# Keys and queries of two batches turned by the DMA crossbar, four PSUM slots in the first MLP pass, and output matmuls handed out in another order

## The chip, the core and the metric

The kernel runs on one core of one Trainium2 chip. The core's engines each work through their own list of instructions in order, and wait for each other by semaphores: PE (TensorE, matmuls and transposes by matmul), DVE (VectorE), ACT (ScalarE), POOL (GpSimd, here mostly an issuer of DMAs and a helper for squares and copies) and SP (SyncE, an issuer of DMAs). The metric is the device time of one execution in microseconds; lower is better. Times quoted as "span" run from the first to the last instruction of the profiled execution.

## What is computed

Two stages, one after the other. First a chunked attention over k, q, v of shape (4 batches, 8 heads, 768 positions, 64): each chunk of 32 positions looks at 16 positions to its left, at itself, at 8 to its right, and at 8 memory positions of its batch and head. Then a two-layer MLP on the 3072 rows of 512 that come out:

```python
for c in range(nc):                       # chunks of 32, nc = 24
    k_full = concat([mem_k, k[max(0, 32c-16) : 32c+40]])
    scores = q_c @ k_full.T / sqrt(64)
    a = softmax(scores)
    out[32c : 32c+32] = a @ v_full
x = out.transpose(0, 2, 1, 3).reshape(3072, 512)
h = x @ w_in                              # 512 -> 2048
g = h + sin(alpha * h)**2 / alpha
return g @ w_out                          # 2048 -> 512
```

## The kernel before

**Layout of the attention.** A batch is worked in eight blocks `j` of 96 query positions (`QW`), that is three chunks. For a block, 120 key positions and the 8 memory keys stand beside each other as 128 columns of `kT` (head dimension on the partitions, two heads stacked). `scores` makes eight matmuls into `sc`, then three exponentials on ACT write `pt` with a mask in the bias; `values` makes eight matmuls with the rows `vw` of v into `ot` and DVE divides by the sum (`rinv`, `x_blk`); `turn_x` transposes the block on PE (`xtp`) and DVE copies it into `xT`. `attention` runs these as a pipeline of steps, with `values` lagging `scores` by `lag` steps, and after each piece takes a given number (`shares`) of matmuls from a `stream`.

**Keys and queries.** `load_qk` brings k and q of a batch as six consecutive positions per partition (`k_bf`, `q_bf`). For batches 1 to 3, POOL pairs two heads (`pair_up`, tile `pr`), PE transposes six 128x128 pieces (`turn`, tiles `tk` and `tq`), and `put_k` (ACT one copy, DVE two) or `put_q` (DVE one copy) spreads them into `kT` or `qT`. There are eight such pieces for a batch, four of k and four of q, numbered `pc`. In the pass of batch 0 they are made at tiles `ft` 8 to 15, in the passes of batches 1 and 2 at every second tile from 2, each for the batch that follows. `put_memk` adds the memory keys, `put_memv` the memory values (eight copies on POOL), `load_v` the rows of v (four DMAs issued by POOL). `kTs`, `qTs` and `vws` have two buffers, used by even and odd batches.

**The MLP.** For a batch there are 16 tiles `ft` of 128 hidden features. `first` makes eight matmuls into `hT`, and ACT takes the sine (`u`). The square `s2` (shown as `s` in the profile) is made on ACT, DVE or POOL: by the string `AVPAVPAVPAVPAVPA` in the first pass, by `AAAV` in the others. `finish` (DVE) writes `gT` and so frees the `hT` slot. `second` is a generator of 96 output matmuls for a batch (six row groups `o` of 16), each group copied to `o_sb` and stored by SP. Those 96 are the `stream`: they are made during the attention and the MLP pass of the next batch, wherever the code takes some.

**PSUM.** Pool `big` has three slots of two banks (for `sc`, `ot`, `hT`), pool `one` two slots of one bank (for `tk`, `tq`, `xtp`, `o`). A tile waits for its slot until the last reader of the slot's old tile is done.

**Order.** The schedule is manual: every engine's instructions stand in the order in which the code writes them. So each of the queues is a list fixed in advance, DMAs included, and the order of the code around the change decides what stands behind what. POOL issues nearly all loads, in the order of the code; a load also waits until the eighth load before it has landed.

The passes follow each other as attention 0, pass 0, attention 1, pass 1 and so on; at the end the 96 output matmuls of batch 3 stand alone.

Of the kernel before, what the change touches and what calls it, by code (L numbers as in the profile page):

```python
# [9 lines left out]
P = 128  # L10
QW = 96
NEG = -30000.0
KW = 856
# [6 lines left out]
class Stream:  # L20


    def __init__(self, gen, n):
        self.gen = gen
        self.left = n

    def take(self, n):
        n = min(n, self.left)
        for _ in range(n):
            next(self.gen)  # L30
            self.left -= 1
# [3 lines left out]
def kernel(  # L35
# [27 lines left out]
    xp = ctx.enter_context(tc.tile_pool(name="xp", bufs=2))  # L63
# [3 lines left out]
    big = ctx.enter_context(tc.tile_pool(name="big", bufs=3, space=bass.MemoryType.PSUM))  # L67
    one = ctx.enter_context(tc.tile_pool(name="one", bufs=2, space=bass.MemoryType.PSUM))

    ctx.enter_context(tc.manual_schedule())  # L70

# [8 lines left out]
    memv_st = consts.tile([P, B, H, D], BF, name="memv_st")  # L80
    memkT = consts.tile([P, HP, 32], BF, name="memkT")
# [8 lines left out]
    def alloc_qk():  # L90
        kb = qkst.tile([P, H, 6, D], BF, name="k_bf")
        qb = qkst.tile([P, H, 6, D], BF, name="q_bf")
        return kb, qb

# [18 lines left out]
    def put_memv(b):  # L113
        for h in range(H):
            nc.gpsimd.tensor_copy(  # L115
                vws[b % 2][64:72, h, :, 0:D],
                memv_st[64:72, b, h, :].unsqueeze(1).to_broadcast([NM, NJ, D]),
            )

    def put_memk(b):  # L120
        nc.vector.tensor_copy(  # L121
            kTs[b % 2][:, :, 24:KW].rearrange("p g (j c) -> p g j c", c=104)[:, :, :, 40:40 + NM],
# [3 lines left out]
    def load_w_in(c):  # L126
        nc.gpsimd.dma_start(  # L127
            w_in_sb[:, :, 256 * c:256 * c + 256],
            moe_w_in[:, 256 * c:256 * c + 256].rearrange("(kt p) f -> p kt f", p=P),
        )  # L130
# [9 lines left out]
    def pair_up(src, hp):  # L140
        pr = blk.tile([P, 6, 2, D], BF, name="pr")
# [5 lines left out]
    def turn(src, hp, pr, name):  # L147
        t = one.tile([P, 6, P], BF, name=name, tag="one")
# [33 lines left out]
    def scores(b, j):  # L182
        sc = big.tile([P, 2, 512], F32, name="sc", tag="big")
        for hp in range(HP):
            for e in range(2):
                nc.tensor.matmul(  # L186
                    sc[:, e, QW * hp:QW * hp + QW],
                    kTs[b % 2][64 * e:64 * e + 64, hp, 104 * j:104 * j + P],
# [17 lines left out]
    def values(b, j, pt):  # L206
        ot = big.tile([P, 2, 512], F32, name="ot", tag="big")
# [18 lines left out]
    def turn_x(xT, j, x_blk):  # L226
        xtp = one.tile([P, KT, QW], BF, name="xtp", tag="one")
# [23 lines left out]
    def first(ft, xT, gT, square):  # L251
        hT = big.tile([P, 2, 512], F32, name="hT", tag="big")
# [89 lines left out]
    for c in range(2, 8):  # L342
        load_w_in(c)
# [107 lines left out]
```

## Time and profile before

| | us |
|---|---|
| median of 3 runs (lowest to highest) | 270.76 (269.01 to 272.1) |
| the profiled execution's own time | 268.79 |
| its span | 267.0 |
| busy in the span: PE, DVE, ACT, POOL | 220.6, 145.2, 156.0, 86.7 |
| attention 0 with all loading ahead | 0 to 33.3 |
| pass 0 | 33.3 to 75.2 |
| attention 1, pass 1 | 75.2 to 97.3, 97.3 to 134.2 |
| attention 2, pass 2 | 134.2 to 152.8, 152.8 to 192.6 |
| attention 3, pass 3 | 192.6 to 210.9, 210.9 to 241.6 |
| output matmuls of batch 3 and the last store | 241.6 to 267.0 |

Matmuls overlap in their pipeline, so the busy time of PE overstates what it did, and the distance from one group of matmuls to the next says more than a single duration. The stages are cut at the first matmul of each on PE; the engines overlap at the seams. Mean granted TensorE clock is 0.962.

### The profile page before, as it was taken

How to read it: one execution, taken by the hardware profiler on the slowest of the kernel's cores; microseconds unless marked ns; L12 is line 12 of the kernel's file. 1: busy time of each engine (PE TensorE's matmuls, PEld its weight loads, DVE VectorE, ACT ScalarE, POOL GpSimd, SP SyncE). 2: the span in 40 equal slices, each digit the busy share in tenths (PEclk: the TensorE clock that was granted, in tenths of full speed). 3: DMA queues.
4: the chain of work that ended last, by engine and by line, in shares of the span. 5: the costliest groups of instructions: out<-in, count | busy, mean ns of one | idle time of the engine just before them, and what ended most of it. 6: DMA issues, size and time to landing. Idle time of an engine off the chain costs nothing.

```text
span 267.0 us, 4449 instructions
## 1 busy us (share of the span) xinstructions
PE 220.6 (83%) x1756; PEld 124.3 (47%) x1781; DVE 145.2 (54%) x271; ACT 156.0 (58%) x238; POOL 86.7 (32%) x114
## 2 busy tenths in 40 slices
PE   1745792297899999898499899999499999999994
PEld 1534551154545555454245555555245555554441
DVE  4524931457983656768727538675747465575100
ACT  2263753057577647977756487778657479773000
POOL 8879745545699201229820011210000000000000
PEclk9999979579999999999979999999979999999999
DMA  6999999999059990108997110110101111011222
GB/s 95 167 131 132 164 202 206 199 95 32 0 62 216 150 116 2 39 0 120 166 130 52 41 42 0 39 42 0 39 2 39 42 39 39 2 41 39 82 79 79
DMA packets 52037, 21.10 MB, mean 79 GB/s; under 512 B 34592, under 2 KB 48944, under 8 KB 52016
## 3 DMA queue, kind: packets, MB, share of 16 engines
q0 software_dynamic: 48240, 14.45, 81.7%
q1 hardware_dynamic: 3776, 6.37, 7.1%
q8 instruction: 14, 0.23, 0.4%
q14 instruction: 7, 0.06, 0.1%
HBM read 28.95 MB, written 6.29 MB: 132 GB/s over the span
## 4 chain that ended last, share of the span: by engine, by line
PE 58%; DVE 11%; POOL 9%; DMA 9%; ACT 7%; issue 4%; ACTq 0%; DVEq 0%; POOLq 0%
PE o L284 28%; PE hT L255 23%; DVE gT L273 6%; DMA q_bf<-in_q_dram 6%; POOL vw L115 3%; DMA vw<-in_v_dram 3%; PE sc L186 3%; ACT u L262 2%; ACT kT L161 2%; DVE qT L173 2%; PE xtp L229 2%; PE ot L212 2%; POOL w_in_sb L127 2%; POOL q_bf L97 1%; DVE kT L167 1%
## 5 line engine op out<-in xcount | busy, mean ns | idle before, releaser
L255 PE MATMUL hT<-xT,w_in_sb 128*128 128x384 bf16 x512 | 96.7, 335 | 15.5 <-DVE gT L273 15.1
L284 PE MATMUL o<-w_out_sb,gT 128*128 128x512 bf16 x359 | 98.1, 387 | 2.1 <-DVE o_sb L292 0.5
L262 ACT ACTIVATE u<-hT,alpha_sb 128x768 f32<-128x768 f32 x64 | 57.6, 900 | 48.3 <-PE hT L255 47.6
L273 DVE SCALAR_TENSOR_TENSOR gT<-s,inv_alpha,hT 128x768 bf16<-128x768 f32 x64 | 63.1, 1008 | 29.6 <-ACT s L267 16.6
L255 PEld LDWEIGHTS <-w_in_sb 128*128 128x128 bf16 x512 | 49.4, 100 | 55.1 <-issue 18.2
L199 ACT ACTIVATE pt<-sc,biasm 128x256 bf16<-128x256 f32 x96 | 38.3, 474 | 26.2 <-PE sc L186 26.0
L284 PEld LDWEIGHTS <-gT 128*128 128x128 bf16 x384 | 33.8, 98 | 30.2 <-issue 0.5
L267 ACT ACTIVATE s<-u 128x768 f32<-128x768 f32 x42 | 35.5, 845 | 1.0
L142 POOL COPY pr<-q_bf 128x768 bf16<-128x768 bf16 x12 | 9.9, 827 | 53.4 <-PE tk L151 50.2
L218 DVE RECIPROCAL rinv<-ot 96x8 f32<-96x8 f32 x32 | 6.5, 202 | 30.6 <-PE ot L212 30.3
L219 DVE TENSOR_TENSOR x_blk<-ot,rinv 96x512 bf16<-96x512 f32 x32 | 22.0, 686 | 1.1
L292 DVE COPY o_sb<-o 128x512 f32<-128x512 f32 x12 | 8.3, 690 | 21.2 <-PE o L284 21.0
L294 ACT COPY o_sb<-o 128x512 f32<-128x512 f32 x12 | 7.0, 586 | 21.5 <-PE o L284 13.1
L212 PE MATMUL ot<-vw,pt 128*128 128x65 bf16 x256 | 14.8, 204 | 5.5 <-POOL vw L115 3.1
L186 PE MATMUL sc<-qT,kT 64*128 64x96 bf16 x256 | 12.2, 226 | 8.3 <-DVE kT L121 8.3
L212 PEld LDWEIGHTS <-pt 128*128 128x128 bf16 x256 | 13.0, 104 | 12.9 <-DMA vw<-in_v_dram 3.5
L115 POOL COPY vw<-memv_st 8x512 bf16<-8x512 bf16 x32 | 18.0, 606 | 0.1
L161 ACT COPY kT<-tk 128x672 bf16<-128x672 bf16 x16 | 11.4, 715 | 9.9 <-PE tk L154 9.6
L173 DVE COPY qT<-tq 128x768 bf16<-128x768 bf16 x16 | 15.3, 954 | 3.4 <-PE tq L151 3.2
L167 DVE COPY kT<-tk 128x48 bf16<-128x48 bf16 x32 | 5.1, 202 | 21.7 <-ACT kT L161 21.7
L270 DVE TENSOR_TENSOR s<-u 128x768 f32<-128x768 f32 x17 | 16.2, 955 | 0.1
L142 POOL COPY pr<-k_bf 128x768 bf16<-128x768 bf16 x12 | 10.5, 876 | 14.3 <-PE tq L151 14.1
(49 smaller groups left out, 138.6 us busy)
## 6 DMA issues: line engine op xcount, KB each, us to landing
out_dram<-o_sb SPq DMA_DIRECT2D x24, 256.0 KB, 2.0
k_bf<-in_k_dram POOLq DMA_DIRECT2D x3, 768.0 KB, 7.5
q_bf<-in_q_dram POOLq DMA_DIRECT2D x3, 768.0 KB, 12.4
vw<-in_v_dram POOLq DMA_DIRECT2D x6, 384.0 KB, 18.8
w_in_sb<-in_moe_w_in_dram POOLq DMA_DIRECT2D x8, 256.0 KB, 7.1
w_out_sb<-in_moe_w_out_dram POOLq DMA_DIRECT2D x4, 512.0 KB, 18.7
k_bf<-in_k_dram POOLq DMA_DIRECT2D x4, 192.0 KB, 5.1
q_bf<-in_q_dram POOLq DMA_DIRECT2D x4, 192.0 KB, 5.4
```

The lines of the kernel that those rows point to most:

```text
L115: nc.gpsimd.tensor_copy(vws[b % 2][64:72, h, :, 0:D], memv_st[64:72, b, h, :].unsqueeze(1).to_broadcast([NM, NJ, D]),)
L142: nc.gpsimd.tensor_copy(pr[:].rearrange("p r e d -> p e r d"), src[:, 2 * hp:2 * hp + 2])
L173: nc.vector.tensor_copy(qTs[b % 2][:, hp, :].rearrange("p (a r) -> p a r", r=6), t[:].rearrange("p r a -> p a r"),)
L186: nc.tensor.matmul(sc[:, e, QW * hp:QW * hp + QW], kTs[b % 2][64 * e:64 * e + 64, hp, 104 * j:104 * j + P], qTs[b % 2][64 * e:64 * e + 64, ...
L199: nc.scalar.activation(pt[:, 0:H * QW].rearrange("p (g e c) -> p g e c", g=2, e=4)[:, :, :, 32 * m:32 * m + 32], sc[:, :, 0:4 * QW].rearra ...
L212: nc.tensor.matmul(otv[:, e, hp, :], pt[:, QW * i:QW * i + P], vws[b % 2][:, 2 * hp + e, j, 0:D + 1],)
L219: nc.vector.tensor_tensor(out=x_blk[:].rearrange("p g e d -> p e g d"), in0=otv[0:QW, :, :, 0:D], in1=rinv[:].unsqueeze(3).to_broadcast([Q ...
L255: nc.tensor.matmul(hT[:, hf, 0:HALF], w_in_sb[:, kt, P * ft:P * ft + P], xT[:, kt, HALF * hf:HALF * hf + HALF], start=(kt == 0), stop=(kt ...
L262: nc.scalar.activation(u[:], hT[:, :, 0:HALF], ACTF.Sin, scale=alpha_sb[:, ft:ft + 1])
L267: nc.scalar.activation(s2[:], u[:], ACTF.Square)
L273: nc.vector.scalar_tensor_tensor(out=gT[:, ft, :].rearrange("p (e c) -> p e c", e=2), in0=s2[:], scalar=inv_alpha[:, ft:ft + 1], in1=hT[:, ...
L284: nc.tensor.matmul(o[:], gT[:, ft, P * s:P * s + P], w_out_sb[:, ft, :], start=(ft == 0), stop=(ft == FT - 1),)
```

## The change

It has four parts.

1. **k and q of batches 2 and 3 no longer pass PE.** `load_rows` (POOL) brings the rows that each block needs into `kst` (16 DMAs and one copy of the memory keys) and q into `qst` (6 DMAs). `cross` then issues 14 DMA transposes from SP, each 128 partitions by 512 elements, into `kT` (now with a pitch of 128 columns to a block) and `qT`. `pair_up`, `turn`, `put_k`, `put_q` and `put_memk` remain for batches 0 and 1.
2. **Four PSUM slots of two banks until the end of pass 0**, for all tiles (`two` and `single` hand out the same pool); after it the old pools `big` and `one` are opened in the same banks.
3. **Batch 1's transposes stand behind pass 0**, alternating with three output matmuls of batch 0 each. `put_memv` of batches 0 and 1 becomes one copy on DVE each, and `load_v(1)` is issued at tile 9 of pass 0. `w_in` comes in 5 loads and not in 8.
4. **Output matmuls are handed out in another order.** A `Feed` strings batches together. Counts before: 16 ahead of attention 1 and 52 in it, 28 in pass 1, 46 in attention 2, 50 in pass 2, 46 in attention 3, 50 in pass 3, 96 at the end. Counts after: 24 between batch 1's transposes, 45 in attention 1, 11 in pass 1, 50 in attention 2, 46 in pass 2, 50 in attention 3, 62 in pass 3, 96 at the end. `lag` is 2 in all attentions. `xT` has one buffer and not two, and `pr` takes its three buffers from those of `u`.

The core of the diff:

```diff
-KW = 856
+KW = 1024
...
+    def load_rows(b):
+        for j in range(NJ):
+            lo = QW * j - 16
+            r0 = max(0, -lo)
+            nc.gpsimd.dma_start(
+                kst[r0:64, j, :].rearrange("p (h d) -> p h d", d=D),
+                k[b, :, lo + r0:lo + 64, :].rearrange("h p d -> p h d"),
+            )
...
+        nc.gpsimd.tensor_copy(
+            kst[64:72], memk_st[64:72, b - 2, :].unsqueeze(1).to_broadcast([NM, NJ, H * D])
+        )
+        for t in range(NSUB):
+            nc.gpsimd.dma_start(
+                qst[:, t, :].rearrange("p (h d) -> p h d", d=D),
+                q[b, :, P * t:P * t + P, :].rearrange("h p d -> p h d"),
+            )
+
+    def cross(b):
+        for j in range(NJ):
+            nc.sync.dma_start_transpose(kTs[b % 2][:, :, P * j:P * j + P], kst[:, j, :])
+        for t in range(NSUB):
+            nc.sync.dma_start_transpose(qTs[b % 2][:, :, P * t:P * t + P], qst[:, t, :])
...
-        rest = stream.left
-        prs = {}
+        rest = max(0, feed.left() - (0 if last else 16))
+        taken = 0
...
-            stream.take(rest * (ft + 1) // FT - (rest - stream.left))
-            if not last and ft >= 2 and (ft >= 8 or i > 0):
...
+            n = rest * (ft + 1) // FT - taken
+            feed.take(n)
+            taken += n
+            if i == 0 and ft == 6:
+                put_memv(1, nc.vector, 0, H)
+            if i == 0 and ft == 9:
+                load_v(1, 0, H)
+            if i > 0 and not last and ft == 2:
+                cross(i + 1)
...
+        feed.add(second(i, gT), NSUB * FT)
+        if i == 0:
+            opened.__exit__(None, None, None)
+            banks["big"] = ctx.enter_context(tc.tile_pool(name="big", bufs=3, space=bass.MemoryType.PSUM))
+            banks["one"] = ctx.enter_context(tc.tile_pool(name="one", bufs=2, space=bass.MemoryType.PSUM))
+            pr = pair_up(kq1[0], 0)
+            for pc in range(2 * HP):
+                nxt = pair_up(kq1[(pc + 1) % 2], (pc + 1) // 2) if pc < 7 else None
+                feed.take(3)
+                t = turn(None, pc // 2, pr, "tk" if pc % 2 == 0 else "tq")
+                (put_k if pc % 2 == 0 else put_q)(1, pc // 2, t)
+                pr = nxt
+            put_memk(1)
         if not last:
...
             if i + 2 < B:
-                kq1 = alloc_qk()
-                load_qk(i + 2, kq1, 0, H)
+                load_rows(i + 2)
             if i == 0:
-                stream.take(16)
-                xT = attention(1, stream, (4, 6, 6, 6, 5, 5, 5, 5, 4, 4, 2), 2)
+                xT = attention(1, feed, (4, 6, 5, 4, 4, 4, 4, 4, 4, 3, 3), 2)
             else:
-                xT = attention(i + 1, stream, (6, 4, 4, 4, 4, 4, 4, 4, 6, 6), 1)
+                xT = attention(i + 1, feed, (10, 8, 4, 4, 3, 3, 3, 3, 4, 4, 4), 2)
```

Three places in the order of the instructions. The first is POOL between the last loads of the weights and pass 0; `vw_88` is v of batch 1 (`vw_85` after), and each `s_...` is a square for pass 0. Before:

```order
L133 DMA w_out_sb<-in_moe_w_out_dram 128x4x512 x4
L106 DMA vw_88<-in_v_dram 48x64x64
L107 DMA vw_88<-in_v_dram 48x64x64
L109 DMA vw_88<-in_v_dram 16x63x64
L111 DMA vw_88<-in_v_dram 8x63x64
L115 COPY vw_88<-memv_st 8x8x64 x8
L270 TENSOR_TENSOR s_615<-u 128x768
L270 TENSOR_TENSOR s_657<-u 128x768
L142 COPY pr<-k_bf 128x2x6x64
```

And in the changed kernel:

```order
L181 DMA w_out_sb<-in_moe_w_out_dram 128x4x512 x4
L396 DMA memk_st<-in_mem_k_dram 8x8x64
L398 DMA memk_st<-in_mem_k_dram 8x8x64
L319 TENSOR_TENSOR s_597<-u 128x768
L319 TENSOR_TENSOR s_639<-u 128x768
L319 TENSOR_TENSOR s_682<-u 128x768
L154 DMA vw_85<-in_v_dram 48x64x64
L155 DMA vw_85<-in_v_dram 48x64x64
L157 DMA vw_85<-in_v_dram 16x63x64
L159 DMA vw_85<-in_v_dram 8x63x64
L319 TENSOR_TENSOR s_728<-u 128x768
```

Three squares of pass 0 now stand ahead of the loads of v, and the eight copies of the memory values are gone from between them.

The second is DVE in the middle of pass 1. `tk` and `tq` are the transposed keys and queries of batch 2. Before:

```order
L292 COPY o_sb<-o 128x512
L167 COPY kT_83<-tk 128x48 x2
L273 SCALAR_TENSOR_TENSOR gT<-s_1353,inv_alpha,hT 128x768
L273 SCALAR_TENSOR_TENSOR gT<-s_1369,inv_alpha,hT 128x768
L270 TENSOR_TENSOR s_1400<-u 128x768
L173 COPY qT_85<-tq 128x768
L273 SCALAR_TENSOR_TENSOR gT<-s_1400,inv_alpha,hT 128x768
L273 SCALAR_TENSOR_TENSOR gT<-s_1417,inv_alpha,hT 128x768
L167 COPY kT_83<-tk 128x48 x2
```

And in the changed kernel:

```order
L319 TENSOR_TENSOR s_1323<-u 128x768
L322 SCALAR_TENSOR_TENSOR gT<-s_1323,inv_alpha,hT 128x768
L322 SCALAR_TENSOR_TENSOR gT<-s_1337,inv_alpha,hT 128x768
L322 SCALAR_TENSOR_TENSOR gT<-s_1352,inv_alpha,hT 128x768
L322 SCALAR_TENSOR_TENSOR gT<-s_1367,inv_alpha,hT 128x768
L319 TENSOR_TENSOR s_1381<-u 128x768
```

The copies that spread `tk` and `tq` no longer stand between two `gT`; their matmuls are gone from PE in the same way, and the one copy for each `tk` from ACT.

The third is SP's whole list, which issues the stores of the result. Before:

```order
L446 UNCONDITIONAL_BRANCH
L304 DMA memk_f<-in_mem_k_dram 8x8x64 x4
L305 DMA alpha_rows<-in_moe_alpha_dram 16x128
L295 DMA out_dram<-o_sb 128x512 x24
L446 UNCONDITIONAL_BRANCH
```

And in the changed kernel:

```order
L354 DMA alpha_rows<-in_moe_alpha_dram 16x128
L344 DMA out_dram<-o_sb 128x512 x4
L139 DMA_TRANSPOSE kT_80<-kst 128x4x128 x8
L141 DMA_TRANSPOSE qT_82<-qst 128x4x128 x6
L344 DMA out_dram<-o_sb 128x512 x4
L139 DMA_TRANSPOSE kT_81<-kst 128x4x128 x8
L141 DMA_TRANSPOSE qT_83<-qst 128x4x128 x6
L344 DMA out_dram<-o_sb 128x512 x16
```

The 14 transposes for batch 2 stand between the fourth and the fifth store, those for batch 3 between the eighth and the ninth.

More of the change, by code (lines that the diff above doesn't have):

```diff
@@ L17, with __init__, add, left @@
 ALU = mybir.AluOpType
[L20 to L25, printed above, removed]
-    def take(self, n):
[L28 to L31, printed above, removed]
+class Feed:
+    def __init__(self):
+        self.parts = []
+    def add(self, gen, n):
+        self.parts.append([gen, n])
+    def left(self):
+        return sum(p[1] for p in self.parts)
+    def take(self, n):
+        while n > 0 and self.parts:
+            p = self.parts[0]
+            next(p[0])
+            p[1] -= 1
+            n -= 1
+            if p[1] == 0:
+                self.parts.pop(0)
 @with_exitstack
```

107 lines of the change are left out of this document (51 added, 56 removed).

## The prediction

> **What bounds the kernel now.** I read the page's slices first: where is PE idle, and does its clock suffer? Each digit is a fortieth of the span, 6.7 us.
>
> ```profile
> PE   1745792297899999898499899999499999999994
> PEclk9999979579999999999979999999979999999999
> DMA  6999999999059990108997110110101111011222
> ```
>
> PE is the fullest engine but not always: it is poor in slices 0 to 7, dips at slices 19 and 28, and its granted clock falls right behind such holes (slices 5, 7, 20, 29). The next view is the busy time of each engine by stage (length; then PE, PEld, DVE, ACT, POOL; clock; DMA).
>
> ```profile
> 0.00:33.30 33.30, 17.30 (x261) 12.89 (x262) 16.65 (x65) 14.86 (x30) 28.33 (x45) 0.99 1.65 138
> 33.30:75.20 41.90, 28.98 (x181) 16.83 (x180) 21.94 (x32) 20.19 (x25) 23.46 (x26) 0.84 1.68 117
> 97.30:134.20 36.90, 30.55 (x209) 17.62 (x212) 24.70 (x35) 27.79 (x35) 16.52 (x21) 1.00 0.76 70
> 152.80:192.60 39.80, 35.72 (x232) 19.90 (x235) 25.32 (x36) 29.02 (x36) 4.14 (x5) 1.00 0.07 27
> 210.90:241.60 30.70, 30.54 (x172) 17.00 (x174) 18.61 (x21) 23.90 (x28) 0.00 (x0) 1.00 0.07 26
> ```
>
> These are the load stage and the four MLP passes. Pass 3 has no transposes and is full: 30.7 us with 50 output matmuls. Passes 1 and 2 do about the same work in 36.9 and 39.8, pass 0 takes 41.9 with no output matmuls at all. Why pass 0 is slow stands in its waits and its chain.
>
> ```profile
> PE hT L255 <- DVE gT L273: 12.9, 7, 9.2
> DVE gT L273 <- POOL s L270: 12.1, 2, 9.7
> POOL vw L111 <- DMA q_bf<-in_q_dram: 3.1, 1, 3.1
> ...
> 43.72 0.69 POOL vw L111
> 44.54 4.50 POOL vw L115 x8
> 49.12 1.48 POOL s L270
> 50.62 1.02 DVE gT L273
> 51.69 7.83 PE hT L255 x32
> ```
>
> One wait of 9.2 us: PE lacks a slot, because DVE lacks a square, because POOL stands at a load of v (held by an earlier load's landing) and then at eight copies, ahead of that square in its list. After it, 32 matmuls take 7.83 us; eight take 1.30 at full clock:
>
> ```profile
> 154.77 1.30 PE hT L255 x8
> 156.07 0.65 PE o L284 x3
> 245.35 10.74 PE o L284 x49
> 74.76 0.34 PE tq L151 x6
> ```
>
> So a tile of `hT` costs PE 1.30 us, an output matmul 10.74/49 = 0.219, six transposes 0.34. Passes 1 and 2 show the other loss: PE waits for DVE behind the transposes' copies in each pair of tiles, and at the end for `kT`.
>
> ```profile
> 113.16 1.47 PE hT L255 x8
> 121.51 1.47 PE hT L255 x8
> ...
> 133.84 0.34 PE L186 MATMUL sc<-qT,kT 64*128 64x96 bf16 x8 [4.02 <-DVE kT L121]
> 191.65 0.22 DVE L121 COPY kT<-memkT 128x256 bf16<-128x256 bf16 x1
> 191.92 0.34 PE L186 MATMUL sc<-qT,kT 64*128 64x96 bf16 x8 [3.50 <-DVE kT L121]
> ```
>
> In pass 1 four tiles take 121.51 - 113.16 = 8.35 us, and attentions 2 and 3 begin with 4.02 and 3.50 us of waiting; the clock's dip of slice 20 follows the first.
>
> **The change part by part.** I go through the changed program in time, with the profiled execution's span of 267.0 as the base.
>
> *Up to 33.3 us.* Unchanged. The memory values of batch 0 become one DVE copy of 8x4096; by the 0.22 us of a 256-element copy above, sixteen times that is 3.5 us (from below near nothing, since few of those elements were contiguous). It is hidden, because `values` waited for v itself:
>
> ```profile
> 22.95 0.51 PE L212 MATMUL ot<-vw,pt 128*128 128x65 bf16 x6 [2.31 <-DMA vw<-in_v_dram]
> ```
>
> The loads fill the DMA slices 1 to 9, and their order ahead of v is the same. `w_in` is issued earlier but stands behind the same bytes. One pool of four slots for all tiles: `ot` waits for the `sc` four tiles back, three back before; the same tile in steady state. 0 us.
>
> *Pass 0, 33.3 to 58.4.* The 9.2 us wait goes (squares stand ahead of the loads of v), with it the slow clock, and eight transposes with their copies.
>
> ```profile
> 33.00:36.00 3.00, 2.96 (x13) 1.62 (x14) 0.77 (x3) 0.00 (x0) 1.49 (x2) 0.50 1.37 196
> 37.95 1.01 DVE L273 SCALAR_TENSOR_TENSOR gT<-s,inv_alpha,hT 128x768 bf16<-128x768 f32 x1 [3.85 <-ACT s L267]
> 68.56 0.93 DVE gT L273
> 66.82 0.87 DVE s L270
> L270 POOL TENSOR_TENSOR s<-u 128x768 f32<-128x768 f32 x5 | 8.3, 1667 | 11.9 <-ACT u L262 11.8
> ```
>
> PE needs 16 x 1.30 = 20.8 plus 1.3 for a first tile at half clock: 22.1, the floor. DVE comes late next: from its first `gT` at 37.95, 16 x 0.93 + 5 x 0.87 + 3.5 for the memory values = 22.7, so its last `gT` ends near 60.7; PE's last tile ends two to three tiles before, near 58. The four loads of v in POOL's list now stand ahead of the square of tile 11 and cost some of the fourth slot's slack: 0.4. I take 25.1 (22.1 to 30, the upper end if each of the five POOL squares at 1.67 stalls a tile).
>
> *Batch 1's transposes, 58.4 to 70.0.* Now exposed, but filled: eight times 3 x 0.219 + 0.34 = 1.0 us, 8.0. Ahead of them the new pools wait for the last `gT` of the old slots (sine, square and `gT` behind the last tile): 2.2. Behind them `qT`, the memory keys and the first `scores`: 0.95 + 0.22 + 0.2 = 1.4. Together 11.6 with 24 output matmuls; before, the same stretch was 75.2 to 78.66, 3.5 us with 16.
>
> *Attention 1, 70.0 to 87.0.*
>
> ```profile
> 78.66 0.34 PE L186 MATMUL sc<-qT,kT 64*128 64x96 bf16 x8
> 97.13 1.47 PE L255 MATMUL hT<-xT,w_in_sb 128*128 128x384 bf16 x8
> ```
>
> It took 18.5 us with 52 output matmuls, so 18.5 - 52 x 0.219 = 7.1 for itself; with 45 it is 17.0.
>
> *Pass 1, 87.0 to 111.5.* PE has 16 x 1.30 + 11 x 0.219 = 23.2. What is late next is ACT:
>
> ```profile
> 98.64 0.90 ACT L262 ACTIVATE u<-hT,alpha_sb 128x768 f32<-128x768 f32 x1 [1.22 <-PE hT L255]
> 101.98 0.88 ACT L262 ACTIVATE u<-hT,alpha_sb 128x768 f32<-128x768 f32 x1
> ```
>
> These are the first and the third sine of the pass, two tiles apart: a tile with both sine and square on ACT takes (101.98 - 98.64)/2 = 1.67 us, one with the sine alone after about 0.92: (3 x 1.67 + 0.92) x 4 = 23.7. Three engines this near each other disturb each other: 24.5 (23.2 to 28). The wait of 4.0 at the end goes, since `kT` comes by DMA.
>
> *The rest.* Attention 2 with 50: 7.1 + 50 x 0.219 = 18.0, to 129.5. Pass 2 with 46: 20.8 + 46 x 0.219 = 30.9, to 160.4. Attention 3: 18.0, to 178.4. Pass 3: 30.7 with 50, so 33.3 with 62, to 211.7. The end as before, 25.4: **237.1**.
>
> The sum by its differences: pass 0 -16.8, transposes +8.1, attention 1 -1.5, pass 1 with its wait -12.2, attention 2 -1.0, pass 2 with its wait -8.2, attention 3 -0.9, pass 3 +2.5, together -30. Half of it is idle time of pass 0, most of the rest the stalls of passes 1 and 2; 16 x 0.34 = 5.4 us of transposes is work removed from PE. The profiled execution took 268.79 and lies 2 us below the median of 270.76; the median less 30 is **241**.
>
> **The cover of the new loads.** That sum holds only if `kT` and `qT` are there in time.
>
> ```profile
> q0 software_dynamic: 10304, 2.56, 173.5%
> DMA  0000969999999999999999999999999992800000
> L111 POOL DMA_DIRECT2D vw<-in_v_dram x5 | 3.9, 773 | 3.3 <-DMA q_bf<-in_q_dram 3.1
> vw<-in_v_dram POOLq DMA_DIRECT2D x4, 192.0 KB, 8.2
> out_dram<-o_sb SPq DMA_DIRECT2D x24, 256.0 KB, 2.0
> ```
>
> The first two lines are the loads of k, q and v of batch 3, in the window 119 to 147: 10,304 packets in 30 busy slices of 0.7 us, 2.0 ns each. `load_rows` moves pieces of one head of one position: 936 rows of k and 768 of q, times 8 heads, 13,632 pieces, so 27 us. POOL can begin near 66, when its last `pr` is out. Its 22 issues at 0.77 and the copy of 8x4096 (4.5, as the eight copies of 8x512 in the chain above) take 22 us, so POOL is through near 90 and the data has landed near 95; v follows by 115, where `values` needs it near 119. The gap behind the copies on POOL costs nothing: no square stands there in passes 1 and 2.
>
> SP can begin the transposes near 85, after the fourth store. The first is needed at 111.5, the last by step 6 of attention 2, near 123 (six steps of 7.1/8 and 32 output matmuls later): free up to (123 - 85)/14 = 2.7 us each, one after another. For batch 3 SP is past its eighth store near 129.5, the last is needed near 172: 3.0 us each. No row shows a transpose. From below, 512 pieces of 256 bytes at 2.0 ns are 1.0 us; the nearest row of like shape is a store from SP, 2.0 to landing; from above, a load of 192 KB that landed after 8.2 us in a full queue, scaled to 128 KB, 5.5 each. I take the store's 2.0: 28 us for a batch, hidden. Behind the transposes on SP stand only stores; the fifth is due near 111.
>
> The Trainium skill speaks against this part and for it. "VectorE: DVE Perf Modes", section "The three transpose paths", gives 1309 ns for a 128x128 bf16 transpose by the DMA crossbar against 390 on TensorE; four to an instruction would be, as an estimate, 5.2 us, and the sum would come to 307. "Advanced Engine Details and Errata", section "X-Bar Transpose (TRN2)", says such DMAs are as fast as regular ones, which would leave the sum as it is. No trace here shows either.
>
> **Rivals.** *Other engines bind sooner (250).* The floors of PE, DVE and ACT in passes 0 and 1 lie within 2 us of each other. At the upper ends above pass 0 gains 5 less and pass 1 3.5 less: 241 + 8.5. For it: POOL's squares wait 11.8 us for ACT, and DVE's memory copy has no row. Against: pass 3 runs full with the same chain.
>
> *Transposes late, slower than before (315).* SP works its list in order; at 5.5 us each attention 2 waits 14 x (5.5 - 2.7) = 39 and attention 3 14 x (5.5 - 3.0) = 35 us: 241 + 74. It decides from 2.7 us on, and at 28x = 30 + 14 x 2.7 + 14 x 3.0, x = 3.9, the gain is gone; between them it costs 0 to 30. By the first figure from the Trainium skill's "VectorE: DVE Perf Modes", this is the case that would come. Against, in the rows: the store's 2.0 and 1.0 from the pieces, and DMAs overlap.
>
> *The loads come late (255), so the cover is not what it says.* At twice the price of a piece, q lands near 121 rather than 95, attention 2 waits some 10 us, attention 3 a few. For it: the pieces are small and many, and v shares the queue. Against: v's own pieces are in the 2.0 ns.
>
> **How the numbers follow.** The forecast, 241, gets 0.64 and spans 235 (the DVE copy at nothing, PE's floor in pass 1) to 246. Engines binding sooner: 0.16. Transposes late, but faster than before: 0.05; at or over 3.9 us, 0.08. Loads late: 0.04. Nothing comes of it for a reason I don't see: 0.03. Over 1%, about what a measurement of this kernel can tell from no change, gives faster 0.88, within 0.02, slower 0.10. The range that leaves out two in ten reaches from 233 to 258: it takes in the forecast's bounds, the second case and most of the late loads.
>
> **What would show it.** Right: pass 0 near 25 us with no PE wait over 2 us; six-matmul groups of `pr` only between 58 and 70; pass 1 near 24.5 with ACT nearly full; no PE wait at the first `scores` of batches 2 and 3; SP's transposes ended before 113 and 172. Wrong: PE waiting at L235 for a DMA into `kT` or `qT`, or DVE waiting for POOL's squares in pass 0. The forecast fails most if a transpose holds SP for over 3.9 us.

## The result, and the profile after

The changed kernel took **246.49 us** (245.26 to 247.55, four runs) against 271.35 (269.01 to 272.1) for the kernel before in the same session: a ratio of **0.9096**, 95% interval 0.9016 to 0.9175, a gain of 24.9 us. Forecast were 241 and a gain of 30, with a range of 233 to 258. The profiled execution has a span of 245.8 us against 267.0, and a mean granted clock of 0.986 against 0.962; it is the slowest of the four runs (247.55). Four executions on record, one each of the kernel before (291.02) and of the experiments with the crossbar undone (315.38), with the transposes in pass 0 (438.65) and with four slots longer (434.54), were far slower than the others of their kernel and count in no ratio.

The page's slices first, as before the change: busy tenths of PE, the granted clock, the DMA engines' share.

```profile
PE   1560989978698998999998999999989999999993
PEclk9999999999589999999999999999999999999999
DMA  6999999989909999999999999931111011102212
```

PE's holes at slices 6, 7, 19 and 28 (counted from 0) are gone, and with them the clock's dips at slices 5, 7, 20 and 29. One new dip stands at slices 10 and 11 (61 to 74 us), where batch 1's transposes now are. The DMA engines, nearly free before at slices 15 to 17 and from 22 on, are now busy from slice 12 to 25, with `load_rows` and the loads of v.

The view by stage of the changed kernel follows (window; its length; then busy time of PE, PEld, DVE, ACT, POOL; granted clock; DMA share; GB/s). The windows are attention 0, pass 0, the stretch of batch 1's transposes, attention 1, pass 1, attention 2, pass 2, attention 3, pass 3, the end.

```profile
0.00:35.60 35.60, 18.13 (x262) 13.84 (x262) 18.39 (x68) 14.83 (x30) 23.67 (x36) 1.00 1.92 149
35.60:60.33 24.73, 22.96 (x131) 13.03 (x129) 19.42 (x21) 17.17 (x20) 10.59 (x9) 1.00 1.82 158
60.33:75.76 15.43, 10.72 (x73) 6.27 (x73) 8.70 (x18) 5.90 (x7) 11.16 (x14) 0.78 1.20 41
75.76:92.36 16.60, 16.30 (x205) 9.21 (x206) 9.67 (x24) 10.68 (x26) 16.56 (x19) 1.00 1.32 111
92.36:119.24 26.88, 24.31 (x143) 13.46 (x142) 16.97 (x18) 23.75 (x28) 16.28 (x24) 1.00 2.29 131
119.24:137.54 18.30, 17.32 (x212) 9.71 (x212) 13.07 (x28) 13.00 (x30) 16.82 (x18) 1.00 1.66 148
137.54:168.36 30.82, 30.82 (x178) 16.91 (x176) 17.84 (x19) 25.42 (x30) 4.43 (x8) 1.00 1.78 113
168.36:186.66 18.30, 17.32 (x212) 9.72 (x212) 13.07 (x28) 12.63 (x29) 0.00 (x0) 1.00 0.12 45
186.66:220.14 33.48, 33.48 (x191) 18.29 (x189) 18.59 (x21) 25.17 (x29) 0.00 (x0) 1.00 0.09 32
220.14:245.80 25.66, 21.58 (x101) 9.59 (x98) 4.74 (x6) 3.20 (x5) 0.00 (x0) 1.00 0.20 72
```

Pass 0 fell from 41.4 us (to the end of its last `hT`) to 24.7, pass 2 with its wait from 39.3 to 30.8, and PE is busy for all of passes 2 and 3. Two stages are not full: the stretch of the transposes, at a clock of 0.78, and pass 1, where PE is busy for 24.3 of 26.9 us.

What PE waits for (us in all, times, longest); the rows left out belong to the loads at the start or stay below 1.6 us in all:

```profile
PE hT L304 <- DVE gT L322: 4.3, 7, 1.2
PE o L333 <- DVE gT L322: 3.5, 1, 3.5
PE sc L235 <- DVE kT L168: 2.2, 2, 1.2
```

The 9.2 us wait of pass 0 is gone, and so are the waits of 4.02 and 3.50 for the memory keys ahead of attentions 2 and 3; the two that are left in the last row belong to batches 0 and 1. New is one wait of 3.5 us of an output matmul for the last `gT` of pass 0. No wait for a DMA into `kT` or `qT` appears. SP's queue shows why: its DMAs in order, start and time until the next of another kind.

```profile
91.70 14.23 SPq L139 DMA_TRANSPOSE kT<-kst  x8
106.03 11.88 SPq L141 DMA_TRANSPOSE qT<-qst  x6
120.06 17.61 SPq L344 DMA_DIRECT2D out_dram<-o_sb  x4
137.85 14.10 SPq L139 DMA_TRANSPOSE kT<-kst  x8
152.06 8.27 SPq L141 DMA_TRANSPOSE qT<-qst  x6
```

Batch 2's 14 transposes take 26.2 us (1.87 each), batch 3's 22.5 (1.6 each). The first scores of the two batches stand at 119.24 and 168.36.

### The profile page after: what moved, and what is told of

Same layout as the page of the kernel before. It is cut to its first block, busy times and chain, and to the rows that moved or that the text cites. A ratio compares the mean times of both kernels' runs of the same rounds, so it can differ in the third digit from the quotient of the medians.

```text
span 245.8 us, 4362 instructions
## 1 busy us (share of the span) xinstructions
PE 213.0 (87%) x1685; PEld 120.0 (49%) x1685; DVE 140.5 (57%) x249; ACT 151.8 (62%) x230; POOL 99.5 (40%) x123
## 4 chain that ended last, share of the span: by engine, by line
PE 61%; POOL 14%; DVE 9%; DMA 7%; ACT 4%; issue 3%; DVEq 0%; POOLq 0%; ACTq 0%
PE o L333 29%; PE hT L304 23%; DVE gT L322 4%; DMA vw<-in_v_dram 4%; DMA q_bf<-in_q_dram 3%; PE ot L261 3%; PE sc L235 3%; POOL kst L124 2%; POOL kst L119 2%; ACT u L311 2%; POOL qst L132 2%; PE xtp L278 2%; DVE s L319 2%; POOL kst L128 1%; DVE x_blk L268 1%
## 5 line engine op out<-in xcount | busy, mean ns | idle before, releaser
L333 PE MATMUL o<-w_out_sb,gT 128*128 128x512 bf16 x384 | 103.2, 385 | 5.8 <-DVE gT L322 3.5
L304 PE MATMUL hT<-xT,w_in_sb 128*128 128x384 bf16 x512 | 92.8, 330 | 4.3 <-DVE gT L322 4.3
L322 DVE SCALAR_TENSOR_TENSOR gT<-s,inv_alpha,hT 128x768 bf16<-128x768 f32 x64 | 63.9, 1012 | 35.0 <-ACT s L316 32.6
L304 PEld LDWEIGHTS <-w_in_sb 128*128 128x128 bf16 x512 | 50.3, 99 | 43.3 <-issue 8.3
L209 ACT COPY kT<-tk 128x672 bf16<-128x672 bf16 x8 | 5.7, 718 | 19.2 <-PE tk L202 10.0
L124 POOL DMA_DIRECT2D kst<-in_k_dram x16 | 11.8, 740 | 9.1 <-DMA vw<-in_v_dram 7.8
L319 POOL TENSOR_TENSOR s<-u 128x768 f32<-128x768 f32 x5 | 7.8, 1566 | 14.4 <-ACT u L311 14.4
L278 PE MATMUL xtp<-ident,x_blk 96*128 96x96 bf16 x128 | 12.1, 223 | 1.0 <-DVE x_blk L268 1.0
L278 PEld LDWEIGHTS <-x_blk 96*128 96x128 bf16 x128 | 9.3, 106 | 7.5 <-DVE x_blk L268 1.7
L281 DVE COPY xT<-xtp 128x384 bf16<-128x384 bf16 x32 | 11.1, 346 | 2.6 <-PE xtp L278 2.6
## 6 DMA issues: line engine op xcount, KB each, us to landing
vw<-in_v_dram POOLq DMA_DIRECT2D x6, 384.0 KB, 11.4
```

The lines of the kernel that those rows point to most:

```text
L124: nc.gpsimd.dma_start(kst[72:72 + n, j, :].rearrange("p (h d) -> p h d", d=D), k[b, :, QW * j + 48:QW * j + 48 + n, :].rearrange("h p d -> ...
L278: nc.tensor.transpose(xtp[:, kt, :], x_blk[:, kt].rearrange("p e d -> p (e d)"), ident[0:QW, 0:QW])
L304: nc.tensor.matmul(hT[:, hf, 0:HALF], w_in_sb[:, kt, P * ft:P * ft + P], xT[:, kt, HALF * hf:HALF * hf + HALF], start=(kt == 0), stop=(kt ...
L319: eng.tensor_tensor(out=s2[:], in0=u[:], in1=u[:], op=ALU.mult)
L322: nc.vector.scalar_tensor_tensor(out=gT[:, ft, :].rearrange("p (e c) -> p e c", e=2), in0=s2[:], scalar=inv_alpha[:, ft:ft + 1], in1=hT[:, ...
L333: nc.tensor.matmul(o[:], gT[:, ft, P * s:P * s + P], w_out_sb[:, ft, :], start=(ft == 0), stop=(ft == FT - 1),)
```

## The experiments

Each kernel is the changed one with the edit shown; the edits are shortened, and words behind `...` or in place of code say what stands there. Differences in us between experiments are between medians of different sessions, in which the kernel before took 270.2 to 271.5, so they are good to about 1 us. The stages below are cut in the profile of each kernel at the first `hT`, the end of the last `hT` of pass 0 ("transposes" runs from there), and the first `sc` and `hT` behind it.

| us | before | after | no crossbar | old pass 0 | last version |
|---|---|---|---|---|---|
| attention 0 | 33.3 | 35.6 | 35.0 | 35.7 | 35.1 |
| pass 0 | 41.4 | 24.7 | 25.3 | 43.5 | 24.5 |
| transposes | 3.9 | 15.4 | 14.1 | 5.9 | 10.4 |
| attention 1 | 18.5 | 16.6 | 16.6 | 16.6 | 16.4 |
| pass 1 | 36.7 | 26.9 | 38.4 | 26.9 | 25.9 |
| attention 2 | 18.8 | 18.3 | 20.8 | 18.3 | 18.3 |
| pass 2 | 39.3 | 30.8 | 40.7 | 30.8 | 30.8 |
| attention 3 | 18.8 | 18.3 | 20.8 | 18.3 | 18.3 |
| pass 3 and end | 56.3 | 59.2 | 58.9 | 59.2 | 59.1 |

### The crossbar undone

```diff
-            if i > 0 and not last and ft == 2:
-                cross(i + 1)
+            if i > 0 and not last and 2 <= ft < 18 and ft % 2 == 0:
+                ... pair_up, turn (slot of one bank), put_k / put_q as in the kernel before
-                load_rows(i + 2)
+                kq1 = alloc_qk()
+                load_qk(i + 2, kq1, 0, H)
```

> k and q of batches 2 and 3 come as in the kernel before, through TensorE in passes 1 and 2; everything else is the changed kernel's. My theory, that the crossbar part is worth the waits of 4.0 and 3.5 us ahead of attentions 2 and 3, the 16 x 0.34 = 5.4 us of transposes and the stalls behind their copies: +14 to +18 us, 261 to 265, with a PE wait for DVE's memory keys at the first scores of batches 2 and 3. Rival, that the stalls of passes 1 and 2 came from the old order of the output matmuls: only the 5.4 us and little of the waits come back, +5 to +8, 252 to 255.

It took 272.35 us, ratio to the kernel before 1.0063 (1.0027 to 1.01). That is +26 on the changed kernel, more than either theory gave: **the whole gain is gone**. The stages are those of a second run of the same kernel.

> The same kernel as the first experiment, for a profile of its stages. Theory, that passes 1 and 2 carry the 26 us that it lost: 37 to 40 us each in place of 26.9 and 30.7, with stalls behind the transposes' copies and 3.5 to 4 us ahead of the scores. Rival, that part of it stands elsewhere, in the attentions or in pass 0 at a lower clock: passes 1 and 2 below 36.

271.73 us, ratio 1.003 (0.9989 to 1.0071). Its view by stage, from pass 1 to the end of attention 3:

```profile
91.05:129.44 38.39, 27.37 (x191) 15.63 (x188) 24.64 (x35) 28.35 (x34) 13.28 (x16) 0.98 0.36 38
129.44:150.25 20.81, 19.83 (x210) 10.38 (x211) 9.58 (x24) 10.99 (x27) 3.76 (x7) 0.87 2.59 122
150.25:190.91 40.66, 34.79 (x228) 19.22 (x225) 25.18 (x36) 29.44 (x35) 6.61 (x8) 0.98 0.07 27
190.91:211.71 20.80, 19.82 (x211) 10.37 (x212) 9.58 (x24) 10.99 (x27) 0.00 (x0) 0.87 0.07 27
```

Pass 1 lost 11.5 us, pass 2 9.9: the first theory's place. The attentions lost 2.5 each, which neither theory had, and there the clock column reads 0.87 in place of 1.00. The chain behind it, in the trace from the last tiles of pass 1 on, DVE first:

```profile
125.36 1.00 DVE L322 SCALAR_TENSOR_TENSOR gT<-s,inv_alpha,hT 128x768 bf16<-128x768 f32 x1
...
127.27 1.02 DVE L322 SCALAR_TENSOR_TENSOR gT<-s,inv_alpha,hT 128x768 bf16<-128x768 f32 x1
128.20 0.95 DVE L221 COPY qT<-tq 128x768 bf16<-128x768 bf16 x1
129.06 0.32 DVE L168 COPY kT<-memkT 128x256 bf16<-128x256 bf16 x1
```

```profile
129.44 0.50 PE L235 MATMUL sc<-qT,kT 64*128 64x96 bf16 x8 [4.88 <-DVE kT L168]
```

The last `qT` copy stands on DVE behind the whole tail of the pass, so PE waits for 4.88 us, and what follows runs at 0.50 us for eight small matmuls where 0.34 is the time at full clock. With the crossbar the keys and queries of attention 2 do not depend on DVE's list any more.

The numbers that place the output matmuls make it worse. This kernel has 11 of them in pass 1, where the kernel before had 28, and yet four tiles in the middle of the pass take the same time, 116.76 - 108.41 = 8.35 us here and 8.35 before:

```profile
108.41 1.47 PE L304 MATMUL hT<-xT,w_in_sb 128*128 128x384 bf16 x8 [1.03 <-DVE gT L322]
116.76 1.48 PE L304 MATMUL hT<-xT,w_in_sb 128*128 128x384 bf16 x8 [0.81 <-DVE gT L322]
```

So the 17 that are gone had cost next to nothing there, in PE's stalls. They stand now where PE is busy: four more in each of attentions 2 and 3 and twelve more in pass 3, which is, at 0.219 each, about 4.4 us (pass 3 and the end are 2.6 longer than before). Pass 1 as a whole is 1.7 longer than the old one (38.4 against 36.7), and that stands at its head: ACT loads the table for the sine at 92.59, behind the first `hT`, where the kernel before had done so ahead of it, at 96.13 with `hT` from 97.13 on:

```profile
96.13 1.28 ACT L262 ACT_TABLE_LOAD   x1
```

### Pass 0 undone, in parts and whole

POOL's order, then three and two slots, then the place of the transposes, then all three.

```diff
-            if i == 0 and ft == 6: put_memv(1, nc.vector, 0, H)
-            if i == 0 and ft == 9: load_v(1, 0, H)
+    load_v(1, 0, H)             # behind load_w_out, ahead of attention 0
+    for h in range(H):
+        put_memv(1, nc.gpsimd, h, h + 1)
```

> The loads of batch 1's v and eight copies of its memory values stand on POOL ahead of the squares again; the rest is the changed kernel's. My theory, that half of the gain was one wait of PE for a POOL square behind these rows, of which a fourth slot of PSUM covers one tile of 1.3 us: pass 0 grows by 8 us and some of its clock is lost, +8 to +11, 254 to 257. Rival, that four slots and transposes moved out of the pass give enough slack: +0 to +3, up to 250.

257.85 us, ratio 0.953 (0.9489 to 0.957): +11.4. The timeline in pass 0 of this kernel:

```profile
48.50 4.50 POOL L162 COPY vw<-memv_st 8x512 bf16<-8x512 bf16 x8
53.09 1.47 POOL L319 TENSOR_TENSOR s<-u 128x768 f32<-128x768 f32 x1
...
55.66 6.63 PE L304 MATMUL hT<-xT,w_in_sb 128*128 128x384 bf16 x25 [9.86 <-DVE gT L322]
```

The old wait is back, 9.86 us where the kernel before had 9.2: four slots and no transposes in the pass did not shorten it. Behind it 25 matmuls take 6.63 us, 0.265 each, where full clock gives 1.30/8 = 0.163. Pass 0 took 35.75 (+11.0) at a clock of 0.86.

```diff
-    opened = tc.tile_pool(name="four", bufs=4, space=bass.MemoryType.PSUM)
+    banks["big"], banks["one"]: 3 slots of two banks and 2 of one, from the start
```

> PSUM has three slots of two banks and two of one from the start, as in the kernel before; the rest is the changed kernel's. My theory: in pass 0 a tile with its square on POOL holds a slot for about 1.3 + 0.9 + 1.7 + 1.0 = 4.9 us against 3 x 1.3 = 3.9 of three slots, so five tiles lose 1.0 each, +5; the wait of 3.5 us for the old slots at batch 1's transposes and the half clock behind it (1.5) go, -5: 245 to 248 in all, 246.5. Rival, that the fourth slot is what the change lives on: pass 0 returns to 33 us or more, 252 to 256. Second rival, that it was worth nothing in pass 0: 241 to 243.

247.25 us, ratio 0.914 (0.9104 to 0.9176): the same as the changed kernel, as the theory's two halves say. Pass 0 took 29.1 (+4.4), the stretch of the transposes 10.6 (-4.8), at a clock of 1.00. **The fourth slot gained 4.4 us in pass 0 and gave them back** where the old pool is closed.

```diff
+            if i == 0 and ft >= 8:
+                ... pair_up, turn, put_k / put_q of piece ft - 8, slots of the four
...
-                ... eight times feed.take(3) and a piece
+            feed.take(24)
```

> Batch 1's transposes stand in the second half of pass 0 again, between the tiles, out of the four slots; the 24 output matmuls that were put between them come in one piece ahead of attention 1. My theory, that the move by itself costs as much as it brings (transposes are 8 x 0.34 = 2.7 us of PE wherever they stand): pass 0 +4 to +6, the stretch behind it 15.4 - 5, in all -1 to +1, 245.5 to 247.5. Rival, that a transposed tile takes a slot from hT and POOL's pairing stands ahead of squares: pass 0 +9 or more, 250 to 254.

253.23 us, ratio 0.9349 (0.931 to 0.9388): +6.7, the rival's number. Pass 0 grew by 9.4 to 34.2, at a clock of 0.91, and the stretch behind it fell by 3.6 to 11.8. The rows of POOL show where, and it is not quite where the rival had it:

```profile
52.94 1.40 POOL L154 DMA_DIRECT2D vw<-in_v_dram  x1
...
56.43 0.82 POOL L159 DMA_DIRECT2D vw<-in_v_dram  x1
57.25 0.84 POOL L190 COPY pr<-k_bf 128x768 bf16<-128x768 bf16 x1
```

```profile
58.14 0.75 PE L199 MATMUL tk<-ident,pr 128*128 128x128 bf16 x6 [3.81 <-POOL pr L190]
```

A `pr` stood behind the four loads of v, and PE, in order, behind that `pr`. In the changed kernel these loads stand in the same place, but no `pr` follows them, and no wait of PE in pass 0 exceeds 0.9 us. The rival's two reasons, slots taken from `hT` and squares behind POOL's pairing, show little: the waits of `hT` for `gT` come to 1.4 us.

> The other half of the change undone: three slots and two from the start, batch 1's v and memory values on POOL ahead of the squares, batch 1's transposes between the tiles of pass 0; the crossbar for batches 2 and 3 and the numbers that place the output matmuls stay (24 of them in one piece ahead of attention 1). By the stages: pass 0 returns from 24.7 to about 41.9 and the stretch behind it from 15.4 to 24 x 0.219 + 1.5 = 6.8: +8.6, 255. Rival, that pass 0's part is worth nothing, since without the crossbar the kernel gained nothing with it: 246.5. Second rival, that the loads of batch 2's rows now start later and the crossbar with them, so that attention 2 waits: 258 or more.

With all three undone 257.03 us, ratio 0.9484 (0.944 to 0.9528): +10.5, near the 255 of the first theory. Pass 0 took 43.5, the stretch 5.9; its waits of `hT` for `gT` are 15.5 us, the longest 10.9. The three together cost no more than POOL's order alone (+11.4). The late-crossbar rival fell: pass 1 and both later attentions are to 0.1 us those of the changed kernel.

So the halves of the change cost 10.5 (pass 0) and 25 to 26 (crossbar) when each alone is undone, together some 11 us more than the 24.9 they bring. The output matmuls are placed for a kernel that has both; by the estimate above that is about 4.4 of the 11, and the slow clock of attentions 2 and 3 another part. No run undid the crossbar together with the placement, so the split is not shown.

### Each transpose twice

```diff
-            nc.sync.dma_start_transpose(kTs[b % 2][:, :, P * j:P * j + P], kst[:, j, :])
+            for _ in range(2): the same       # and for qTs
```

> Each transpose by the DMA crossbar is issued twice, so that SP has 28 instead of 14 for a batch. My theory, that SP works them one behind the other at 14.2/8 = 1.8 and 2.0 us each and that the cover of batch 2 is about 1.3 us: k of batch 2 ends near 91.7 + 28.4 = 120.1, q near 144, while its last tile is needed near 131: +12 in attention 2; batch 3 some +4: 258 to 264. Rival, that the second of a pair overlaps with the first on the queue, so that SP's time is issue and not the transfer: +0 to +3, 247 to 250.

317.05 us, ratio 1.1739 (1.1666 to 1.1812): +70.6, far above both. Its SP queue, and PE's waits:

```profile
90.98 45.92 SPq L140 DMA_TRANSPOSE kT<-kst  x16
136.96 26.90 SPq L143 DMA_TRANSPOSE qT<-qst  x12
163.91 12.31 SPq L346 DMA_DIRECT2D out_dram<-o_sb  x4
176.38 37.10 SPq L140 DMA_TRANSPOSE kT<-kst  x16
213.53 22.52 SPq L143 DMA_TRANSPOSE qT<-qst  x12
```

```profile
PE sc L237 <- DMA qT<-qst: 45.1, 6, 25.3
PE o L335 <- DVE o_sb L343: 15.9, 3, 14.5
```

A tile now holds SP for (45.92 + 26.90)/14 = 5.2 us for batch 2 and (37.10 + 22.52)/14 = 4.3 for batch 3, more than twice the 1.87 and 1.6. The second of a pair writes what the first has written, and the median from issue to landing is 2.6 us, near the 2.87 from one to the next: they go one by one, where in the changed kernel a landing takes 10.1 (k) at 1.78 from one to the next, so they overlap. So this run nearly trebles the price and does not double it; what it shows is what the price decides. The prediction's rival gave 315 at 5.5 us a transpose; 5.2 and 4.3 gave 317. Its mechanism is right, its sum (35 + 18 = 53 at these prices) too small: two costs it lacks are the stores queued behind the transposes on SP (the 15.9 us), and the clock (0.69 from 137 to 164 us).

### The stretch behind pass 0

In the changed kernel's trace the head of this stretch reads:

```profile
63.85 1.44 PE L333 MATMUL o<-w_out_sb,gT 128*128 128x512 bf16 x3 [3.52 <-DVE gT L322]
...
65.08 0.84 PE L199 MATMUL tk<-ident,pr 128*128 128x128 bf16 x6
...
70.48 0.81 PE L333 MATMUL o<-w_out_sb,gT 128*128 128x512 bf16 x3
...
71.13 0.50 PE L199 MATMUL tk<-ident,pr 128*128 128x128 bf16 x6
```

After the wait of 3.52 us the same groups take 1.44 and 0.84, and six microseconds later 0.81 and 0.50. Five of the experiments leave this stretch as it is (POOL's order, the crossbar undone, each transpose twice, pass 1's squares, the start). PE waits 3.5 to 3.6 us there in each, and the stretch takes 14.0 to 15.6: what differs is how long the slow groups last. In the start experiment, with 14.0, the first two pieces behind the wait take 3.24 us (64.61 to 67.85) in place of 1.97, and from then on the clock is full; in the changed kernel three pieces take 5.65 in place of 3.0.

```diff
-            opened.__exit__(...); big = 3 slots, one = 2 slots    # ahead of the pieces
-                feed.take(3)
+                feed.take((12, 4, 4, 4, 2, 2, 2, 0)[pc])
+            feed.take(2)
+            opened.__exit__(...); big = 3 slots, one = 2 slots    # behind them
```

> The pool of four slots is kept until batch 1's transposes are done, with 12 output matmuls ahead of the first transposes, 18 between the others and 2 behind the last (32 in place of 24; attention 1 has 37 in place of 45). My theory, that the wait of 3.52 us was for all of the old slots at once and the half clock behind it came of that wait: the stretch from pass 0 to the first scores takes 32 x 0.219 + 8 x 0.34 + 1.5 = 11.2 us in place of 15.4, attention 1 loses 8 x 0.219 = 1.8: -5 to -6, 240.5 to 241.5. Rival, that PE then waits for the same last gT, as an output matmul needs it too: -1 to -2, 245.

244.48 us, ratio 0.9012 (0.8967 to 0.9058). By the ratio alone this can't be told from the changed kernel (0.9016 to 0.9175), by the stages it can: the stretch took 11.3 us, with 32 matmuls, at full clock.

```profile
62.24:73.55 11.31, 9.61 (x80) 5.45 (x80) 8.89 (x18) 5.20 (x7) 10.74 (x14) 1.00 1.55 58
73.55:89.54 15.99, 14.51 (x195) 8.45 (x199) 9.67 (x24) 11.05 (x26) 15.95 (x18) 1.00 1.20 114
```

The rival is out: with the old slots kept, PE makes output matmuls at once. That the wait was for the exchange of the pools, and not for want of work ahead of the transposes, shows in the kernel with three and two slots from the start too: its output matmuls come three at a time as in the changed kernel, and PE waits 1.4 us there, for a `pr`, at full clock. Attention 1 gave 0.6 of the expected 1.8; at 37 matmuls PE is busy for 14.5 of 16.0 us, no longer full.

### Pass 1

Two edits for its excess of 2.4 us: squares moved from ACT to DVE, and the tables loaded ahead.

```diff
-            sq = ... else "AAAV"[ft % 4]
+            sq = ... else ("AAVAVAAVAVAAVAVA"[ft] if i == 1 else "AAAV"[ft % 4])
```

> In pass 1 six of 16 squares are on DVE in place of four; the rest is the changed kernel's. My theory, that ACT's chain sets pass 1: ACT does 16 x 0.89 + 10 x 0.84 = 22.6 in place of 24.3 us, the pass falls from 26.9 to 25.2 and the whole to 244.8. Rival, that the late table load at its head (first sine at 2.85 us) sets it, or DVE becomes late: -0.5 to +1, 246 to 247.5.

247.83 us, ratio 0.9168 (0.9138 to 0.9198). Pass 1 took 27.4 us: the rival. ACT's work fell (21.48 us busy against 23.75) and the time did not; ACT now waited 3.8 us in the pass for PE (0.9 before the edit, the first tile left out), so ACT's throughput is not what sets the pass.

```profile
92.05:119.47 27.42, 24.14 (x140) 13.43 (x141) 19.77 (x21) 21.48 (x26) 18.08 (x26) 1.00 2.10 135
```

```diff
+            if s == NJ - 1: nc.scalar.activation(warm[:], biasm[:, 5:6], ACTF.Sin)
...
+            if ft == FT - 1 and not last: nc.scalar.activation(warm[:], biasm[:, 5:6], ACTF.Exp)
```

> A sine of one column is put behind the last exponentials of each attention, and an exponential of one column ahead of the last square of passes 0 to 2, so that ACT loads its tables there. My theory: pass 1's load at 93.91 behind its first tile is the only sine table that is late, 1.28 us; those of the exponentials at attentions 2 and 3 start about 1 us behind the first scores and are covered by output matmuls in part: -1.3 to -2.5, 244 to 245. Rival, that the load is hidden everywhere: 246 to 247.

246.76 us, ratio 0.9131 (0.9075 to 0.9186): no difference in the whole, but two in the stages. Pass 1 fell by 1.3 to 25.6, as the theory says. The head of pass 1 in the changed kernel shows the load that is gone from there:

```profile
92.36 2.77 PE L304 MATMUL hT<-xT,w_in_sb 128*128 128x384 bf16 x16
...
93.91 1.28 ACT L311 ACT_TABLE_LOAD   x1 [2.76 <-PE hT L304]
...
98.08 1.46 PE L304 MATMUL hT<-xT,w_in_sb 128*128 128x384 bf16 x8 [1.22 <-DVE gT L322]
```

The stretch behind pass 0 took 16.3: the exponential's table load stands there ahead of the last square, for whose `gT` the pools wait, and that wait is 4.35 us in place of 3.52. Attention 2 stayed at 18.3, so the exponential's load was hidden.

### The start

```diff
-    for c in range(5): load_w_in(c)
+    load_w_in(0), load_w_in(1), eight put_memv(0, nc.gpsimd, h, h + 1), then load_w_in(2) to (4)
-    put_memv(0, nc.vector, 0, H)
```

> Batch 0's memory values are copied by POOL again, eight copies between the second and the third load of w_in; the rest is the changed kernel's. Theory: v of batch 0 came 2 us later because all five loads of w_in now share the DMA engines with it; the copies on POOL hold three of them back by 4.5 us, and pass 0 begins near 33.3 in place of 35.6: -2, 244.5. Rival, that the start moves from execution to execution (34.2 to 36.8 in seven kernels that load in the same order): pass 0 begins in that span, 245.5 to 247.5.

245.28 us, ratio 0.9022 (0.8982 to 0.9061), not to be told from the changed kernel. Pass 0 began at 36.20, so the order of the loads of `w_in` is, by this one profile, not what delayed v; the theory fell.

### A version that beats both

```diff
-                feed.take(3)
+                feed.take((12, 4, 2, 2, 2, 2, 2, 0)[pc])
+            feed.take(6)           # then the pools are exchanged
+            if s == NJ - 1: nc.scalar.activation(warm[:], biasm[:, 5:6], ACTF.Sin)
```

As in the experiment with four slots longer, attention 1 keeps 37 output matmuls.

> Two edits that each moved their stage are joined: the four slots kept until batch 1's transposes are done (16 matmuls ahead of the first two, 10 between the others, 6 behind the last), and the sine table loaded behind the last exponentials of each attention, without the exponential ahead of the last square. By the stages, 15.4 to 11.3 with 0.6 less of attention 1 and 1.3 less of pass 1, less 0.9 for the wait of 1.59 us that is now covered by matmuls: -5.5 to -7, 239.5 to 241. Rival, that the table load only hides behind another wait of pass 1: -4.5, 242.

**241.89 us** (240.49 to 243.1, six runs), ratio 0.8905 (0.887 to 0.894), below the changed kernel's interval. The stretch took 10.4, pass 1 25.9, each at full clock:

```profile
59.56:69.94 10.38, 9.71 (x80) 5.55 (x79) 8.60 (x18) 5.21 (x7) 10.32 (x13) 1.00 1.89 65
...
86.32:112.18 25.86, 24.25 (x143) 13.45 (x140) 17.24 (x18) 22.48 (x27) 14.60 (x20) 1.00 2.02 122
```

The gain by the medians is 4.6, where the theory had 5.5 to 7 and the rival 4.5, so the number is the rival's. By the stages it is 5.0 in the stretch, 0.2 in attention 1 and 1.0 in pass 1, the theory's places; with 0.5 at the start and 0.3 in pass 0 the spans differ by 7.1, but this profile is of the fastest of the six runs (240.49) and that of the changed kernel of its slowest (247.55).

## Why the prediction was right, point by point

By the medians the gain fell 5 us short of the 30 forecast. The places and the mechanisms of both halves came as forecast, and three terms were too small. The spans: 237.1 forecast, 245.8 measured, the latter in the slowest of the four runs. The difference of 8.7 is +2.3 at the start, +3.8 in the stretch of the transposes, +2.4 in pass 1, and no other stage is off by more than 0.5.

*Up to 33.3 us, "unchanged": wrong by 2.3.* Pass 0 began at 35.60. The first scores were already 0.9 late (16.87 against 15.98), the rest came with v. It isn't the order of `w_in` (the start experiment). The changed kernel and the experiments on it began pass 0 between 34.2 and 36.8, so an execution varies by as much as I missed; but the kernel before has one profile, 33.3, just below all of them, and whether a microsecond belongs to the change stays open. The DVE copy of the memory values took 1.26 us, not 3.5, and was hidden.

*Pass 0, 25.1: right (24.7)*, and for the reason given: the experiment that undoes POOL's order alone brings the wait back. What I did not see is that the fourth slot and the moved transposes were worth nothing without it, and the fourth slot nothing in sum even with it.

*The stretch, 11.6: mis-sized (15.4).* The mechanism, new pools that wait for the last `gT`, was there; I took 2.2 us for it (3.52 measured), and priced what follows at full clock. Three pieces at half clock took 63.85 to 69.50, 5.65 us in place of 3.0. The 1.3 from the wait and the 2.6 from the clock are the whole of it, and the version that keeps the slots has neither. In the experiments that leave the stretch as it is the same term is too small by 2.4 to 4.0.

*Pass 1, 24.5 (23.2 to 28): mis-sized (26.9).* "What is late next is ACT" fell with the moved squares. 1.0 to 1.3 us are the late sine table: I took the head of the pass from the kernel before, where the load came ahead of the first `hT`. And 26.9 less 1.3 is still 1.1 over the forecast; there PE waits for `gT`, with all three slots taken. That the third slot sets it is argued; a fourth one in pass 1 was not tried.

*The crossbar hidden: right.* The price I took, 2.0 us, stands against 1.87 and 1.6. The start was not 85 but 91.7, behind the fourth store, and the deadline was wrongly placed: the queue is in order with k first, so the first scores need nine transposes. From the rows, (119.24 - 91.70)/9 = 3.1 us each was free for those, or 2.2 if the 7.7 us that the ninth took to land are left for it; my 2.7 for the 14 lies between. Of the signs I named, one failed for this: SP was through with batch 2's at 117.9 and not before 113. The Trainium skill's "VectorE: DVE Perf Modes", section "The three transpose paths", gives 1309 ns for 128x128. My scaling of it by four, an estimate of 5.2 us an instruction, does not hold here: the whole 128x512 took SP a median of 1.36 us, and landed after 2.5 to 2.6 when one went at a time. Nearer is the Trainium skill's "Advanced Engine Details and Errata", section "X-Bar Transpose (TRN2)", by which such DMAs are as fast as regular ones, though one at a time 128 KB landed after 2.5 to 2.6 us where a store of 256 KB took 2.2.

*The rivals.* "Other engines bind sooner" (250) happened in pass 1 only, and not by the work of ACT, which I named. "Transposes late" and "the loads come late" did not happen: the last q of batch 2 was issued at 116.0 and landed some 7.7 us later, near 124, while the scores that read it stand at 129.9; and POOL copied 8x4096 in 3.6 us where I had 4.5.

*The sum by differences.* Passes 1 and 2 with their waits were to bring 20.4 and brought 18.3 (36.7 + 39.3 less 26.9 and 30.8); pass 0 with the stretch 8.7, and brought 5.2. That such terms add holds only so far: undone one at a time, the two halves cost 36 us, not 24.9.

## What to carry to other kernels

When a pool of buffers was exchanged for another in this kernel, the first new tile waited for the last of the old ones (3.5 us); put work that needs neither at the seam, or keep the old pool until PE has such work. A copy that the next phase needs should not stand in an in-order list behind the tail of the phase that ends: moving it to an idle queue is worth the wait and the slow clock behind it. And where filler work has been placed by numbers, a part of the change taken away without its placement can look dearer than it was: here some 4 of 26 us by an estimate, which no run has tested.

## What the runs showed of the hardware

- TensorE ran at half its clock behind a wait of 3.5 us as it did behind one of 9: behind 3.52 us the groups took 1.44 and 0.84 in place of 0.81 and 0.50. How long that lasted differs between executions with the same wait: it cost 2.6 us in the changed kernel's profile and 1.3 in the start experiment's, so the wait cost 4.8 to 6.2 in all. Behind waits of 1.2 us (first scores of batch 1, pass 1) no such change shows.
- DMA transposes of 128x512 in one queue overlap: those of k took 10.1 us from issue to landing at 1.78 us from one to the next; forced one by one, they took 2.6 and 2.87.
- A copy of 8 partitions by 4096 elements took DVE 1.26 us and POOL 3.59.
